# Attention and gated MLP on one core: the query projection by seven half-size products, with row blocks in two outer passes

## The chip, the cores and the metric

The kernel runs on one core of one Trainium2 chip. The metric is the device time of one execution in microseconds (us). Each kernel was run several times on the same chip beside the kernel before; "median" is the median of such runs. A ratio is the mean time of one kernel's fast runs over the mean of the other's fast runs of the same rounds, so it is not quite the ratio of the medians quoted. In the profile PE is the matmul engine (TensorE), PEld its weight loads, DVE is VectorE, ACT is ScalarE, POOL is GpSimd and SP is SyncE. "Clock" is the share of full speed that the PE's clock was granted.

## The reference

```python
xn = layernorm(x)                                  # x: (1, 2048, 640) bf16
q  = (xn @ wq)                                     # wq: (640, 32*192): 32 heads of 192
k, v = last 512 rows of the caches                 # 32 heads of 192
p  = softmax(q k^T / sqrt(192));  s = (p v) @ wo   # wo: (6144, 640)
g  = silu((sigmoid(xn @ w_gate) * (xn @ w_up)) @ w_down)   # 640 -> 1536 -> 640
return x + s * g
```

## The kernel before

First comes the gate network for all 2048 rows; its result goes to DRAM (`gB_d`). Then follow attention "runs". A run takes two blocks of 512 rows and one group of four heads. It has two halves: scores (with the query projection of the next run between the score tiles), then PV (with the output projection of the run before between the PV tiles). The head group is the outer loop and the row blocks are inside, so keys, values and weights of a group are loaded once.

Names that the profiles use: `ps_all` is PSUM, the eight banks in which PE's results build up; `hT_sb` is the hidden layer of the gate network; `gB_sb` is a row tile of gates on its way to DRAM and `gBa_sb` the same on its way back; `qp` is a product saved from PSUM; `k_sb` holds sorted keys and `kT` turned ones; `o_st` holds results of PV, which a DMA turns into `oT`; `o_sb` is a tile of output rows, ready for its store.

```python
def stage_q(n, u):                       # one tile of the projection: 20 matmuls = 10 pairs
    ...
    ps = bank2()
    for c in range(NCD):                 # 5 chunks of 128 of the 640 inputs
        for h in range(2):               # both halves of a chunk
            for b, r in enumerate((LO, HI)):      # upper and lower 64 rows of the array at once
                x = xnT if b == h else xnS        # xnS: the halves swapped
                nc.tensor.matmul(ps[:, b, :], lhsT=wq_t[g][r, 2*c+h, u::PC], rhs=x[s][r, c, :], ...)
    nc.vector.tensor_copy(qT_t[n][:, u, :, :], ps)
...
blocks = [(g, s) for g in range(NG) for s in range(NST)]
runs = [[n, n + 1] for n in range(0, last - 1, 2)] + [[last - 1], [last]]
...
def finish(ps, gB_sb, t, d0, d1):        # the last head group: gate, residual, store
    nc.vector.tensor_tensor(ps, ps, gB_sb[:, d], ALU.mult)
    nc.vector.tensor_tensor(o_sb[:, d], ps, acc[t][:, d], ALU.add)
    nc.sync.dma_start(of[t * P:(t + 1) * P, d], o_sb[:, d])
```

The softmax here doesn't subtract the row's maximum and nothing guards it: scores larger than these inputs give would overflow.

## Time and profile before

| | before |
|---|---|
| time, median | 929.75 us (929.44 to 930.16, 4 runs beside the changed kernel) |
| PE busy | 914.6 us, 99% of the span |
| DMA moved | 87.17 MB |
| one steady run (two halves) | 23.4 + 23.8 us |

These rows of the page cut the span into 40 slices. Each digit is the busy share of PE, the granted clock and the DMA share, in tenths.

```profile
PE   8999999999999999999999999999999999999997
PEclk9999999999999999999999999999999999999999
DMA  9534430144425342633454244434342434373655
```

PE has no hole between its ends and the clock stays at 0.9 or more. DMA is mostly near 40%. The list of PE's waits (waited for: us in total, times, longest) is correspondingly short; these are its two longest lines:

```profile
PE ps_all L413 <- DVE o_st L436: 1.4, 3, 0.9
PE ps_all L249 <- DVE warm L244: 1.3, 1, 1.3
```

### The profile page before, as it was taken

What the parts mean: (1) busy time and instruction counts of PE and PEld (TensorE: products, weight loads), DVE (VectorE), ACT (ScalarE), POOL (GpSimd) and SP (SyncE); (2) the same over time, 40 slices, a digit from 0 to 9 for tenths busy, and PEclk for the clock granted to TensorE, in tenths of its full rate; (3) what the DMA queues carried; (4) which work ended last, traced back from release to release, by engine and by line L of the source; (5) the groups of instructions that cost most, each with busy time, mean ns of one, the idle gap of its engine ahead of it and who ended that gap; (6) DMA issues with size and microseconds to landing.
All of it is one profiled execution on the core that took longest, in us unless ns stands there. A gap on an engine that the chain in (4) does not pass through costs nothing. (4 is left out here: it accounts for less than half of the span.)

```text
span 928.1 us, 18098 instructions
## 1 busy us (share of the span) xinstructions
PE 914.6 (99%) x7946; PEld 546.1 (59%) x8025; DVE 450.7 (49%) x639; ACT 302.1 (33%) x340; POOL 129.5 (14%) x170
## 2 busy tenths in 40 slices
PE   8999999999999999999999999999999999999997
PEld 5545445465756565656565656666665656566665
DVE  5443532443545454545454444444454545454477
ACT  4333322245141424242323333232323242424321
POOL 0021100010002000200020002000100010395800
PEclk9999999999999999999999999999999999999999
DMA  9534430144425342633454244434342434373655
GB/s 290 150 91 102 66 100 16 57 66 83 77 60 112 77 78 61 111 78 68 70 99 90 53 84 81 109 52 87 78 111 52 86 76 113 73 178 77 150 148 148
DMA packets 176960, 87.17 MB, mean 94 GB/s; under 512 B 152241, under 2 KB 171313, under 8 KB 176881
## 3 DMA queue, kind: packets, MB, share of 16 engines
q1 hardware_dynamic: 146864, 47.20, 26.3%
q0 software_dynamic: 6656, 22.81, 10.1%
q10 hardware_dynamic: 23360, 15.99, 6.2%
q8 instruction: 63, 1.03, 0.5%
q14 instruction: 17, 0.13, 0.0%
HBM read 44.70 MB, written 5.24 MB: 54 GB/s over the span
## 5 line engine op out<-in xcount | busy, mean ns | idle before, releaser
L417 ACT ACTIVATE E<-ps_all 128x1024 bf16<-128x1024 f32 x256 | 246.1, 1023 | 487.4 <-PE ps_all L413 372.1
L402 DVE CAST qT<-ps_all 128x1024 bf16<-128x1024 f32 x96 | 117.5, 1225 | 235.9 <-PE ps_all L397 233.4
L474 PE MATMUL ps_all<-wo_g,oT 128*128 128x128 bf16 (+2 forms) x1474 | 224.6, 296 | 3.3
L397 PE MATMUL ps_all<-xnT,wqp 64*128 64x512 bf16 x960 | 222.2, 376 | 0.3 <-DVE o_st L436 0.3
L397 PE MATMUL ps_all<-xnS,wqp 64*128 64x512 bf16 x960 | 221.4, 376 | 0.0
L429 PE MATMUL ps_all<-v_sb,E 128*128 128x193 bf16 x2048 | 190.3, 247 | 0.1
L413 PE MATMUL ps_all<-qT,kT 64*128 64x512 bf16 x1536 | 184.1, 376 | 1.4 <-DVE o_st L436 1.4
L429 PEld LDWEIGHTS <-E 128*128 128x128 bf16 x2048 | 168.5, 98 | 19.3 <-issue 7.2
L474 PEld LDWEIGHTS <-oT 128*128 128x128 bf16 x1536 | 121.5, 98 | 76.5
L397 PEld LDWEIGHTS <-wqp 64*128 64x128 bf16 x1920 | 100.4, 100 | 107.7 <-issue 0.8
L413 PEld LDWEIGHTS <-kT 64*128 64x128 bf16 x1536 | 74.7, 94 | 91.6 <-issue 6.4
L436 DVE TENSOR_TENSOR o_st<-ps_all,rden 128x768 bf16<-128x768 f32 x128 | 122.6, 958 | 8.3 <-DMA oT<-o_st 3.6
L507 DVE TENSOR_TENSOR acc<-ps_all,acc 128x640 f32<-128x640 f32 x96 | 79.2, 825 | 42.7 <-PE ps_all L474 42.7
L131 POOL COPY k_sb<-kn_sb 128x768 bf16<-128x768 bf16 x32 | 25.8, 831 | 273.5 <-DMA kT<-k_sb 225.9
L435 DVE RECIPROCAL rden<-ps_all 128x4 f32<-128x4 f32 x128 | 23.3, 182 | 81.2 <-PE ps_all L429 81.0
L326 DVE TENSOR_TENSOR hT_sb<-ps_all,sig_sb 128x512 bf16<-128x512 f32 x48 | 33.1, 692 | 51.0 <-PE ps_all L320 41.2
L152 POOL DMA_DIRECT2D wqp<-in_A_wq_dram x16 | 11.8, 741 | 319.4 <-PE ps_all L397 270.4
L320 PE MATMUL ps_all<-xnT,wu_sb 128*128 128x512 bf16 x220 | 55.6, 379 | 0.3
L320 PE MATMUL ps_all<-xnT,wg_sb 128*128 128x512 bf16 x220 | 55.5, 379 | 0.3
L340 PE MATMUL ps_all<-wd_sb,hT_sb 128*128 128x128 bf16 (+1 forms) x377 | 52.4, 298 | 0.4
L325 ACT ACTIVATE sig_sb<-ps_all 128x512 bf16<-128x512 f32 x48 | 28.5, 597 | 56.6 <-PE ps_all L320 56.2
L340 PEld LDWEIGHTS <-hT_sb 128*128 128x128 bf16 x384 | 29.7, 98 | 23.1
(49 smaller groups left out, 270.9 us busy)
## 6 DMA issues: line engine op xcount, KB each, us to landing
wqp<-in_A_wq_dram POOLq DMA_DIRECT2D x16, 480.0 KB, 6.4
wo_g<-in_A_wo_dram ACTq DMA_DIRECT2D x8, 960.0 KB, 5.9
kn_sb<-in_A_k_cache_dram POOLq DMA_DIRECT2D x32, 192.0 KB, 4.4
v_sb<-in_A_v_cache_dram ACTq DMA_DIRECT2D x28, 192.0 KB, 3.1
gB_d<-gB_sb POOLq DMA_DIRECT2D x16, 160.0 KB, 2.2
xnS<-xnT SPq DMA_DIRECT2D x8, 320.0 KB, 4.8
gBa_sb<-gB_d POOLq DMA_DIRECT2D x16, 160.0 KB, 2.8
xa_sb<-in_A_x_dram POOLq DMA_DIRECT2D x16, 160.0 KB, 3.1
```

Of the source, the lines that this page charges most:

```text
L320: nc.tensor.matmul(gu[:, i, :], lhsT=w[:, c, f * P:(f + 1) * P], rhs=xnT[s][:, c, :], start=(c == 0), stop=(c == NCD - 1),)
L325: nc.scalar.activation(sig_sb[:], gu[:, 0, :], AF.Sigmoid)
L326: nc.vector.tensor_tensor(hT_sb[:, f, :], gu[:, 1, :], sig_sb[:], ALU.mult)
L340: nc.tensor.matmul(oB_ps[:, d0:d0 + dsz], lhsT=hT_sb[:, f, q * P:(q + 1) * P], rhs=wd_sb[:, f, d0:d0 + dsz], start=(f == 0), stop=(f == NF ...
L397: nc.tensor.matmul(ps[:, b, :], lhsT=wq_t[g][r, 2 * c + h, u::PC], rhs=x[s][r, c, :], start=(c == 0 and h == 0), stop=(c == NCD - 1 and h ...
L402: nc.vector.tensor_copy(qT_t[n][:, u, :, :], ps)
L413: nc.tensor.matmul(ps[:, b, :], lhsT=kT[r, c * PC + j, :], rhs=qT[r, j, pp, :], start=(j == 0), stop=(j == PC - 1),)
L417: nc.scalar.activation(E_t[n, pp][:, c, :, :], ps, AF.Exp, scale=scale_qk)
L429: nc.tensor.matmul(o_ps[:, q // 2, q % 2, 0:DH + 1], lhsT=E[:, c, i, q * P:(q + 1) * P], rhs=vt[:, c, 0:DH + 1], start=(c == 0), stop=(c = ...
L436: nc.vector.tensor_tensor(o_st[:, :, i * DH:(i + 1) * DH].rearrange("p (b i) d -> p b i d", b=2), o_ps[:, :, :, 0:DH], rden[:].to_broadcas ...
L474: nc.tensor.matmul(oA[:, d0 - base:d0 - base + dsz], lhsT=oT_t[n, pp][:, q * PC + j, :], rhs=wo_t[g][:, cc, d0:d0 + dsz], start=(cc == 0), ...
L507: nc.vector.tensor_tensor(acc[t][:], oA[:, 0:D], acc[t][:], ALU.add)
```

## The change

The intent is to save matmuls. Take two row blocks, the two 64-row halves of each input chunk, and the two head pairs of a group. The projection is then a 2x2 by 2x2 block product, and Winograd's scheme does it with seven half-size products in place of eight, at the price of sums of rows (X) and of weights (T). The sums are kept in fp32r, with four bytes an element. The sums of rows have to stay in memory for a whole pass, so the row blocks become the outer loop: two passes of eight head groups.

```diff
+XA, XB, XC = (xnt_pool.tile([P, NCD, 512], FR, ...) for i in "ABC")        # sums of rows, fp32r
+TA, TB, TC = (wq_pool.tile([P, NCD, PC, P], FR, ...) for i in "ABC")       # sums of weights, fp32r
+    def sum_w(g, i, eng, eng2):            # per chunk group: GpSimd sums, one copy on ScalarE
+        tt(TB[:, cs], b(a,1,1), b(a,0,1), ALU.subtract)
+        tt(TA[:, cs], TB[:, cs], b(a,0,0), ALU.add)
+        tt(TC[:, cs], b(a,1,0), TA[:, cs], ALU.subtract)
+        tt(TA[HI, cs], b(HI,0,1), b(HI,0,0), ALU.subtract)
+        nc.scalar.activation(TB[HI, cs], b(HI,1,1), AF.Copy)        # or eng2.tensor_copy
...
-    stage_q: 6 tiles of 10 pairs per run, 6 casts of 128x1024
+    query_slots: 11 slots per run (ten of 5 pairs, one of 3), 12 copies and 11 adds of 128x512
+        s1: products with wb, X1 (bf16)      s2: TA, XA    s3: TB, XB    s4: TC, XC   (fp32r)
...
-blocks = [(g, s) for g in range(NG) for s in range(NST)]
+runs = [(pi, g) for pi in (1, 0) for g in range(NG)]
...
 in the gate network (stores unchanged on GpSimd), after the second row block:
+                for pp in range(G): load_kn((0, pp), pp); sort_k((0, pp)); turn_k((0, pp))
+                sum_w(0, 0, nc.gpsimd, nc.gpsimd); load_raw(0, 2, nc.gpsimd)
+                sum_w(0, 1, nc.gpsimd, nc.gpsimd); sum_w(0, 2, nc.gpsimd, nc.gpsimd)
...
 in every run, between scores and PV:
+            sum_w(g2, 0, nc.gpsimd, nc.scalar); load_raw(g2, 2, nc.scalar)
+            sum_w(g2, 1, nc.gpsimd, nc.scalar); sum_w(g2, 2, nc.gpsimd, nc.scalar)
...
+        if r > 0 and runs[r - 1][1] == NG - 1:
+            for j in range(4): load_gate(r - 1, j)        # nc.scalar, behind the copies above
```

## The prediction

> **What bounds the kernel now.** I read the page first: busy shares, then the costliest groups.
>
> ```profile
> span 928.1 us, 18098 instructions
> ...
> PE 914.6 (99%) x7946; PEld 546.1 (59%) x8025; DVE 450.7 (49%) x639; ACT 302.1 (33%) x340; POOL 129.5 (14%) x170
> ...
> L417 ACT ACTIVATE E<-ps_all 128x1024 bf16<-128x1024 f32 x256 | 246.1, 1023 | 487.4 <-PE ps_all L413 372.1
> L402 DVE CAST qT<-ps_all 128x1024 bf16<-128x1024 f32 x96 | 117.5, 1225 | 235.9 <-PE ps_all L397 233.4
> ...
> L397 PE MATMUL ps_all<-xnT,wqp 64*128 64x512 bf16 x960 | 222.2, 376 | 0.3 <-DVE o_st L436 0.3
> L397 PE MATMUL ps_all<-xnS,wqp 64*128 64x512 bf16 x960 | 221.4, 376 | 0.0
> ...
> L397 PEld LDWEIGHTS <-wqp 64*128 64x128 bf16 x1920 | 100.4, 100 | 107.7 <-issue 0.8
> ...
> L326 DVE TENSOR_TENSOR hT_sb<-ps_all,sig_sb 128x512 bf16<-128x512 f32 x48 | 33.1, 692 | 51.0 <-PE ps_all L320 41.2
> ```
>
> PE works all the time; every other engine mostly waits for it (the last column names PE). A shorter PE stream shortens the kernel only as long as PE keeps waiting for nobody. How long a projection matmul really takes is not the 376 ns of a row, since they overlap; the timeline of one tile of the projection (20 matmuls) shows the pitch:
>
> ```profile
> 404.74 0.59 PE L397 MATMUL ps_all<-xnS,wqp 64*128 64x512 bf16 x2
> 404.96 0.59 PE L397 MATMUL ps_all<-xnT,wqp 64*128 64x512 bf16 x2
> 405.18 0.59 PE L397 MATMUL ps_all<-xnS,wqp 64*128 64x512 bf16 x2
> ...
> 406.69 0.38 PE L397 MATMUL ps_all<-xnT,wqp 64*128 64x512 bf16 x1
> 406.90 1.46 PE L413 MATMUL ps_all<-qT,kT 64*128 64x512 bf16 x12
> 407.11 1.23 DVE L402 CAST qT<-ps_all 128x1024 bf16<-128x1024 f32 x1 [3.39 <-PE ps_all L397]
> ```
>
> From 404.74 to 406.90 ten pairs (upper and lower 64 rows at once) pass: 0.2155 us a pair. The scores that follow issue at once, and VectorE starts 0.21 us later. The windows of a steady run of two blocks show its two halves:
>
> ```profile
> 402.80:426.20 23.40, 23.40 (x217) 10.77 (x216) 8.06 (x7) 13.99 (x15) 1.60 (x2) 1.00 0.31 77
> 426.20:450.00 23.80, 23.59 (x222) 18.00 (x224) 15.01 (x24) 1.40 (x2) 0.00 (x0) 1.00 0.51 93
> ```
>
> Columns: stretch, length, busy PE, PEld, VectorE, ScalarE, GpSimd, clock, DMA. The first half is scores with projection (16 score tiles of 3 pairs, 6 projection tiles), the second is PV with the output projection. In both PE is full, at a clock of 1.00.
>
> **What the Trainium skill says.** "FP8 and Floating Point Precision", TensorE Precision Notes: reduced-precision fp32 is read as 4 bytes and truncated to FP22, while true fp32 takes 4 passes. I take fp32r to be one pass at bf16's pitch; the trace before holds no fp32r. "TensorE: Matmul & The Clock Gate", LDWEIGHTS and Weight-path perf modes: a load takes columns/1.2 GHz, which is 107 ns for 128, and the fast load isn't given to FP32. The bf16 loads agree with a faster one: in the PV half 16 of them go in 1.32 us, about 80 ns each. An fp32r pair needs two loads, estimated from that page at 213 ns, just under the 215.5 ns of its streams: hidden at best. The same page's specification table has ScalarE, VectorE and GpSimd as strict FIFO; the trace doesn't contradict it (ScalarE issues a load at 402.89 and only then starts the run's first exponential, at 403.70), though nothing there shows a blocked queue. "VectorE: DVE Perf Modes", Why PSUM operands drop a tier: fp32 from PSUM is 1x. The trace: 692 ns at 512 elements, 825 at 640.
>
> **The change, part by part.**
>
> Removed. Per run the projection had 6 tiles of 10 pairs, 60. Now there are eleven slots: ten of 5 pairs and a last one of 3 (its fifth chunk has no partner), 53. Over 16 runs 960 pairs become 848; 112 x 0.2155 = 24.1 us less. This is all there is to gain, 2.6%. Scores, PV, output projection and the gate network keep their matmuls.
>
> Added, evictions. 6 casts of 1225 ns become 12 copies and 11 adds of 128x512. At 692 ns that is 15.9 us instead of 7.4 per run, on an engine with 21.8 us in that half. It fits as a sum, but not as a chain. In Winograd's scheme a bank is saved and then accumulated further, so the next slot on the bank must wait. Head thirds 0 and 1 alternate on banks 4/6 and 5/7 and hide this; the last third has no partner. Independent VectorE ops follow at some 0.61 us (an estimate from 640-wide ones of 0.82 us that start 0.74 us apart), dependent ones 0.09 us after the end before; I allow 0.08 us back to PE. A score tile is 0.647 us. Then:
> - second product of the last third: 0.21+0.69+0.08 after the first, one score tile between: 0.34 us wait;
> - third product: two copies, 0.21+0.61+0.69+0.08=1.59, two score tiles (1.29) between: 0.30;
> - fourth: 0.98 against one score tile: 0.34;
> - first PV tile: its second bank waits for a copy and then an add (1.76) against a score tile and half a PV tile (1.31): 0.45.
> - Besides, scores now own banks 0-3 instead of a ring of eight, so the second score tile waits for the last output-projection tile's addition: 1.01 against 0.65: 0.36, in 13 runs.
> 15 x 1.43 + 13 x 0.36 = 26 us. This alone gives back the gain.
>
> Added, start. The first group's eleven slots have no scores between them. Before, the first cast could start only at 168.63, when the last gate store had landed, and PE had queued other banks; now the third slot needs that add. Walking the slots with 0.6 us ScalarE copies I get 18.5 us where there were 13.0: 7 us of waits on 11.4 of work. Then ScalarE's order in the second stage: before the first exponential stand a weight-sum copy, a load that waits for VectorE's four sums (about 4 us), a copy that waits for that load (3 us) and for four more sums (2.3 us), and a table load (1.28 us). The first exponential so comes about 15 us after the end of the prologue, while PE runs dry after two score tiles and one slot: 13.7 us.
>
> Added, beside other work. Weight sums on GpSimd: 12 per run, about 1.6 us for 768 elements (estimate from 1410 ns at 640), with the key sorting 18 us in a second half of 23.7 us: hidden, except in the first run, whose second half has no output projection (10.6 us): 2 us. K, V and wo are loaded twice and wq is loaded some 2.5 times as often: DMA was at 42% on average and goes to 60% or so: hidden. At the change of pass 4.6 MB of sums come back in one second half: 2 us. The x sums lie in the gate network's slack.
>
> Added, end. The last run has 16 score tiles and no projection beside them, before only 8: ScalarE's 0.93 us pitch against 0.65: 4.2 us.
>
> Sum: 929.6 - 24.1 + 26 + 7 + 13.7 + 2 + 2 + 4.2 = 960; I add 4 us for fp32r loads that show after a wait, since the load is then inside the instruction: **964 us**.
>
> **The rivals.**
> 1. *The saving arrives.* If the waits were half of mine and the queues ordered luckily: 929.6 - 24 + 20, about 925. For it: VectorE has 27% free in that half, and two thirds of the slots alternate banks. Against: the 0.98 us chain consists of measured durations. Faster than 911 needs waits under 6 us, which the prologue alone breaks.
> 2. *fp32r is slow.* 38 of 53 pairs per run are fp32r, 608 in all. If loads don't hide or the array takes two cycles a column, each pair costs up to 0.2155 us more: +131 us, about 1090. For it: no fast load for FP32, and 213 of 215.5 ns leaves no room. Against: one pass by the skill's page. Something between (pair of 0.25 us) gives +21, about 985.
> 3. *DMA or GpSimd becomes the bound*, the sums for the run after next not being ready when its second product starts: at 25 us instead of 18 per run about 1 us a run, 980.
>
> **Range and chances.** Bf16 pitch has about 0.65, then 945 to 975; a little slower 0.2, 975 to 1020; twice as slow 0.15. Faster by over 2% (under 911): 0.04. Within 2% (up to 948.2): 0.22, where my waits are half too large. Slower: 0.74. Range 938 to 1030.
>
> **What would show it.** Right: fp32r pairs at 0.216 us, PE busy falling by some 24 us, idle PE rising from 14 us to about 65, released by VectorE in front of the last third's products and the first PV tile; one hole of 10 us or more in the first run's scores with ScalarE waiting for a load; VectorE busy near 590 us (450.7 - 117.5 + 16 x 15.9). Wrong: a pair pitch over 0.23 us (rival 2), PE waiting for GpSimd in every run (rival 3), or VectorE waits under 0.5 us per run, when the time falls under 938.

## The result, and the profile after

The changed kernel takes 1073.58 us (1072.15 to 1075.64, 4 runs) against 929.75 us beside it: ratio 1.1548, 95% interval 1.1528 to 1.1568. It is 144 us slower. The direction was as predicted; the time lies outside the range of 938 to 1030.

The page of the changed kernel, its first lines and the same rows of slices:

```profile
span 1070.4 us, 18623 instructions
...
PE 944.3 (88%) x7706; PEld 607.7 (57%) x7785; DVE 597.6 (56%) x913; ACT 360.1 (34%) x401; POOL 520.8 (49%) x480
...
PE   9988929849799999999999992469999999999995
PEclk9999969869899999999999996679999999999998
...
DMA  8445650242839596696989583682959695984756
```

240 matmuls are gone, yet PE's busy time has risen, and its share fell from 99% to 88%. There are holes in slices 3 to 11 (the gate network and the first runs) and a large one in slices 25 to 27, where the second pass begins. In the slices of the large holes the granted clock is low too.

The list of PE's waits names who ended them, and the windows of one steady run show that the holes are not there (columns: stretch, length, busy PE, PEld, DVE, ACT, POOL, clock, DMA share, GB/s):

```profile
PE ps_all L612 <- DVE o_sb L622: 37.6, 3, 33.6
PE ps_all L555 <- ACT E L559: 19.2, 9, 13.6
PE ps_all L377 <- DVE gB_sb L409: 18.8, 1, 18.8
PE ps_all L555 <- DVE o_sb L622: 8.8, 1, 8.8
PE ps_all L401 <- DVE hT_sb L383: 5.7, 3, 2.5
```

```profile
568.70:592.60 23.90, 23.64 (x204) 14.12 (x202) 15.29 (x23) 14.98 (x15) 5.25 (x6) 1.00 1.05 197
592.60:616.50 23.90, 23.69 (x221) 18.01 (x224) 15.21 (x24) 3.25 (x4) 23.13 (x22) 1.00 0.61 122
```

A steady run takes 47.78 us against 47.23. So the change is nearly neutral there: of the 142 us between the two profiled spans only some 8 lie in eleven steady runs. I read the starts of the stages off PE's timeline in each trace and took differences (us):

| stretch | before | changed | difference | predicted |
|---|---|---|---|---|
| gate network, to the first projection matmul | 164.5 | 195.7 | +31.2 | 0 |
| first projection without scores | 13.0 | 22.9 | +9.9 | 5.5 to 7 |
| run 0 | 35.1 | 54.9 | +19.8 | about 16 |
| run 1 | 48.5 | 54.8 | +6.3 | as a steady run |
| PV of run 8 and scores of run 9 (change of pass) | 47.2 | 100.6 | +53.4 | as a steady run |
| last two runs to the end | 100.2 | 114.3 | +14.1 | 4.2 |
| the rest, eleven steady runs, with the reload of 4.6 MB (+1.5) | 519.6 | 527.2 | +7.6 | small |

**The change of pass.** ScalarE's timeline (start, length, instruction, idle before and what ended it) shows why the first output row of the first pass waited for its gate:

```profile
661.83 0.84 ACT L189 ACTIVATE TB<-raw 64x768 fp32r<-64x768 bf16 x1 [20.31 <-POOL TA L185]
...
671.16 0.84 ACT L189 ACTIVATE TB<-raw 64x768 fp32r<-64x768 bf16 x1 [8.48 <-POOL TA L185]
677.26 0.52 ACT L189 ACTIVATE TB<-raw 64x384 fp32r<-64x384 bf16 x1 [5.26 <-POOL TA L185]
677.32 9.03 ACTq L630 DMA_DIRECT2D gBa_sb<-gB_d  x7
```

The gate loads are issued at 677.3, directly after the third copy. Each copy had waited for a sum of GpSimd, which until 655.3 was preparing output rows. VectorE multiplied the first row by its gate at 679.66, after 36.5 us of idling, and PE, whose PSUM banks were full, went on at 681.48.

**The gate network.** GpSimd's timeline there, then PE's:

```profile
146.03 2.46 POOL L168 DMA_DIRECT2D raw<-in_A_wq_dram  x4
148.48 1.12 POOL L132 DMA_DIRECT2D kn_sb<-in_A_k_cache_dram  x2
149.59 1.08 POOL L411 DMA_DIRECT2D gB_d<-gB_sb  x2
```

```profile
158.86 2.29 PE L377 MATMUL ps_all<-x_odd,wg_sb 128*128 128x512 bf16 x5 [18.82 <-DVE gB_sb L409]
```

Two stores of gate rows were ready at 130.8 at the latest (VectorE's operation on the second began at 129.98 and took 0.82 us) but were issued only at 149.59, since they stood on GpSimd behind key sorting and weight sums. They landed at 158.0, and only then had the third row a free buffer (VectorE went on at 157.99, after 27.2 us). Nor does PE restart at full speed. The ten matmuls from 158.86 took until 163.08, 4.2 us; ten such just before the hole took 2.16 us.

PE also waited 7.8 us for `hT_sb`, all of it in the second row block. VectorE's multiplications stood there behind its first long sum of rows (GpSimd's sum, then VectorE's):

```profile
63.14 5.08 POOL L356 TENSOR_TENSOR XB<-x_even,x_odd 64x2560 fp32r<-64x2560 bf16 x1
63.27 7.64 DVE L359 TENSOR_TENSOR XB<-XA,xe_sw 64x2560 fp32r<-64x2560 f32 x1 [1.62 <-POOL XA L353]
```

VectorE's two other sums of this length took 2.8 us each. The first took 7.64 us, and it began just after GpSimd's second sum and ended 2.7 us after that sum. In the fourth row block it met only the last 0.8 us of GpSimd's and took 3.46 us. So VectorE seems to have stood still in it while GpSimd's sum ran; run 8 shows the same with shorter pieces.

### The profile page after: what moved, and what is told of

Its sections match the earlier page's. It is cut to its first block, busy times and chain, and to the rows that moved or that the text cites. A ratio compares the mean times of both kernels' runs of the same rounds, so it can differ in the third digit from the quotient of the medians.

```text
span 1070.4 us, 18623 instructions
## 1 busy us (share of the span) xinstructions
PE 944.3 (88%) x7706; PEld 607.7 (57%) x7785; DVE 597.6 (56%) x913; ACT 360.1 (34%) x401; POOL 520.8 (49%) x480
## 2 busy tenths in 40 slices
DMA packets 247797, 153.93 MB, mean 144 GB/s; under 512 B 196496, under 2 KB 236176, under 8 KB 246944
## 4 chain that ended last, share of the span: by engine, by line
PE 62%; POOL 14%; DMA 11%; DVE 6%; issue 6%; ACT 1%; SPq 0%; POOLq 0%; ACTq 0%; DVEq 0%
PE ps_all L469 18%; PE ps_all L612 13%; PE ps_all L555 12%; PE ps_all L569 11%; PE ps_all L377 4%; DMA gBa_sb<-gB_d 3%; PE ps_all L401 3%; DMA out_dram<-o_sb 2%; POOL TB L184 2%; DMA gB_d<-gB_sb 2%; POOL acc L604 2%; POOL TA L185 2%; POOL TA L187 2%; POOL TC L186 2%; POOL acc L605 1%
## 5 line engine op out<-in xcount | busy, mean ns | idle before, releaser
L612 PE MATMUL ps_all<-wo_g,oT 128*128 128x128 bf16 (+1 forms) x1380 | 214.9, 298 | 41.0 <-DVE o_sb L622 37.6
L555 PE MATMUL ps_all<-qT,kT 64*128 64x512 bf16 x1536 | 216.0, 385 | 33.6 <-ACT E L559 19.2
L184 POOL TENSOR_TENSOR TB<-raw 128x768 fp32r<-128x768 bf16 (+1 forms) x46 | 78.5, 1708 | 286.4 <-PE ps_all L469 282.6
L569 PEld LDWEIGHTS <-E 128*128 128x128 bf16 x2048 | 170.1, 98 | 22.5 <-issue 8.8
L488 DVE COPY qp<-ps_all 128x512 f32<-128x512 f32 x165 | 109.7, 688 | 88.0 <-PE ps_all L469 87.9
L501 DVE TENSOR_TENSOR qT<-ps_all,qp 128x512 bf16<-128x512 f32 x176 | 116.9, 688 | 57.4 <-PE ps_all L469 44.7
L469 PE MATMUL ps_all<-XA,TA 64*128 64x512 f32 x480 | 75.1, 436 | 6.5 <-DVE qT L501 4.2
L187 POOL TENSOR_TENSOR TA<-raw 64x768 fp32r<-64x768 bf16 (+1 forms) x46 | 78.8, 1713 | 3.6
L469 PE MATMUL ps_all<-XB,TB 64*128 64x512 f32 x480 | 79.0, 430 | 0.7 <-ACT qp L486 0.7
L186 POOL TENSOR_TENSOR TC<-raw,TA 128x768 fp32r<-128x768 bf16 (+1 forms) x46 | 70.3, 1528 | 3.6
L185 POOL TENSOR_TENSOR TA<-TB,raw 128x768 fp32r<-128x768 f32 (+1 forms) x46 | 69.4, 1510 | 3.6
L469 PE MATMUL ps_all<-X,wb 64*128 64x512 bf16 x480 | 63.6, 390 | 0.0
```

Of the source, the lines that this page charges most:

```text
L184: tt(TB[:, cs], b(a, 1, 1), b(a, 0, 1), ALU.subtract)
L185: tt(TA[:, cs], TB[:, cs], b(a, 0, 0), ALU.add)
L186: tt(TC[:, cs], b(a, 1, 0), TA[:, cs], ALU.subtract)
L187: tt(TA[HI, cs], b(HI, 0, 1), b(HI, 0, 0), ALU.subtract)
L469: nc.tensor.matmul(ps_all[:, b, :], lhsT=w(r, c), rhs=x[r, c, :], start=(first and k == 0), stop=(k == len(cs) - 1), skip_group_check=True,)
L488: nc.vector.tensor_copy(dst, part(b))
```

## The experiments

Fourteen runs of thirteen kernels gave results. All were correct. Times are medians in us; the kernel before took 929.84 to 930.10 beside them.

**1. Gate loads on SyncE.**

```diff
-        nc.scalar.dma_start(gates[t][:], gB_d[...])
+        nc.sync.dma_start(gates[t][:], gB_d[...])
```

> Edit: the loads of the saved gate rows (gB_d to gBa_sb) are issued by SyncE and no longer by ScalarE. Theory (in-order queues): in the changed kernel these loads are issued at 677.3 only because they stand on ScalarE behind three weight-sum copies that wait for GpSimd; the first output row of the first pass then waits 36.5 us for its gate and PE 33.6 us for VectorE. With the loads on SyncE that hole should fall to 0 to 12 us, the end should gain some us too, and the time should fall from 1073.6 to about 1040 (1030 to 1050). Rival (the 4.6 MB of sums that come back at the change of pass fill the DMA engines): the hole stays near 33 us and the time within 5 us of 1073.

Measured: 1069.01 (1058.84 to 1069.69). PE's long wait fell from 33.6 to 18.4 us, not below 12, in the profiled execution, which was the fastest (the other three took 1068.6 to 1069.7). The gain in time was only 5 us in the median, so my theory was half right. SyncE's own list of waits for that stretch shows what now stood in front of the gate loads:

```profile
SPq L147 <- POOL k_sb L140: 23.0, 1, 23.0
```

A transpose of keys stood on SyncE ahead of them and waited 23.0 us for keys that GpSimd sorted only after it had prepared the output rows (at 654.6). It was issued at 656.25, and the first gate loads at 658.88. One queue had hidden another.

**2. All gate stores on ScalarE.**

```diff
-                nc.gpsimd.dma_start(gB_d[...], gB_sb[:])
+                nc.scalar.dma_start(gB_d[...], gB_sb[:])
```

> Edit: the stores of the gate rows (gB_sb to gB_d) are issued by ScalarE and no longer by GpSimd. Theory (in-order queues): the gate network ends 31 us later in the changed kernel because the stores of its third and fourth row block stand on GpSimd behind key sorting and weight sums; the buffer gB_sb comes free late, VectorE waits 27 us for it and PE 18.8 us for VectorE, and some 2 us are lost to a lowered clock after it. With the stores on ScalarE the network should end near 171 to 176 us in place of 195.7 (the waits of the second row block, about 8 us, stay) and the time should be 1048 to 1055. Rival (the slowness in that stage comes from VectorE's and GpSimd's x sums or from DMA traffic as such): the end of the network moves by less than 8 us.

Measured: 1076.26, no gain. The 18.8 us wait was gone, but PE now waited 7.0 us for a gate weight at the start and 8.4 and 6.5 us for transposed rows. GpSimd's timeline tells why:

```profile
1.46 3.16 POOL L155 DMA_DIRECT2D v_sb<-in_A_v_cache_dram  x4 [0.16 <-issue]
```

In the changed kernel this load of values was issued at 51.80, behind the fourth gate store. The stores had been holding the attention's loads back. Without them the loads start at 1.5 us, before most of the gate network's own weights.

**3. Only the late gate stores on ScalarE.**

```diff
-                nc.gpsimd.dma_start(gB_d[...], gB_sb[:])
+                (nc.gpsimd if s < 2 else nc.scalar).dma_start(gB_d[...], gB_sb[:])
```

> Edit: the stores of the gate rows of the third and fourth row block are issued by ScalarE; those of the first two stay on GpSimd, where they hold back the loads of keys, values and weights that stand behind them. (With all of them on ScalarE the earlier run showed these loads already at 1.5 us, in front of the gate network's own weights, and new PE waits of 7.0 and 8.4 us for DMAs.) Theory (order on GpSimd's queue, both ways): the 18.8 us wait of PE for gB_sb goes and no wait at the start comes; the last matmul before the projection falls from 195.7 to about 172 to 178 and the time to 1049 to 1057. Rival (stage limited by DMA traffic of the saved sums and key loads): it moves by less than 8 us, with PE waiting for DMAs instead.

Measured: 1054.61, 19 us faster. The gate network ended at 180.0 in place of 195.7, and the first projection took 18.2 in place of 22.9 us, since its second add no longer waited for the last gate store. The end of the network is 2 us later than I expected: 11.0 us of waits for VectorE's `hT_sb` remain, where VectorE does the long sums of rows or waits for GpSimd's.

**4. ScalarE free ahead of the first run's scores.**

```diff
-    for i in range(3):
-        sum_w(1, i, nc.gpsimd if i == 1 else nc.vector, nc.scalar)
-        if i == 0: load_raw(1, 2, nc.scalar)
...
+    sum_w(1, 0, nc.vector, nc.vector)
+    load_raw(1, 2, nc.sync)
+    sum_w(1, 1, nc.gpsimd, nc.gpsimd)
+    # sum_w(1, 2, nc.vector, nc.vector) after the third score tile of run 0
```

> Edit: in front of the first run's scores ScalarE no longer makes copies for the second head group's weight sums nor issues their third load (copies go to VectorE or GpSimd, the load to SyncE); the third sum is emitted after three score tiles. Theory (in-order queue of ScalarE): the 13.6 us in which PE waits for the first exponential fall to under 4 us and the time falls by 7 to 12 us, to about 1064 (some of it comes back because VectorE has more to do there). Rival (the hole comes from the missing queries, that is from VectorE's chain or fp32r products, not from ScalarE's order): the hole stays over 10 us, the time within 3 us of 1073.6.

Measured: 1063.78 (1062.53 to 1068.64), 9.8 us faster. PE's longest wait for an exponential fell from 13.6 to 3.2 us, and the first half of run 0 from 41.4 to 35.0. ScalarE's order was the cause of the hole; part of it came back as a wait of 4.4 us for VectorE, which had been given the copies, and whose second sum now stood among the scores.

**5. Projection slots spread unevenly.**

```diff
-            if done < len(q_list) and (k + 1) * (len(q_list) + 1) >= (done + 1) * len(s_list):
+            if done < len(q_list) and k in (1, 2, 3, 4, 5, 6, 7, 8, 10, 12, 13):
```

> Edit: only the places of the eleven projection slots among the sixteen score tiles change: the first eight directly one after the other, two score tiles ahead of the last third's second product and of its fourth. Theory (VectorE chains of the last third set the waits): the waits there, about 0.7 us per run in the changed kernel, mostly go, and with 15 runs the time falls by 6 to 12 us, to about 1064. Rival (the steady state is lost to fp32r pairs that are slower than bf16 pairs, 0.233 against 0.216 us, and the waits hide under them): the time stays within 4 us of 1073.6, and the pairs keep 0.233 us.

Measured: 1064.98 (1059.12 to 1068.12), 8.6 us faster. A steady run went from 47.78 to 47.25 us. So part of its time was VectorE's chain in the last third. PE's timeline of this run also shows the rival's term side by side, since score tiles (12 matmuls, partly split over two lines) and slots alternate without waits:

```profile
518.34 0.83 PE L555 MATMUL ps_all<-qT,kT 64*128 64x512 bf16 x6
518.98 1.26 PE L469 MATMUL ps_all<-X,wb 64*128 64x512 bf16 x10
520.06 0.83 PE L555 MATMUL ps_all<-qT,kT 64*128 64x512 bf16 x6
520.52 1.53 PE L469 MATMUL ps_all<-XA,TA 64*128 64x512 f32 x10
521.88 0.84 PE L555 MATMUL ps_all<-qT,kT 64*128 64x512 bf16 x6
```

A score tile with a bf16 slot takes 520.06 - 518.34 = 1.72 us, with an fp32r slot 521.88 - 520.06 = 1.82 us. Five fp32r pairs thus cost 0.10 us more: with 0.647 us for the score tile, 0.235 us a pair against 0.2155. Taken from the single starts in this trace, pairs within an fp32r slot follow one another by 0.233 us in the median, and by 0.216 within a bf16 slot.

**6. Preparation and gate loads moved.** The first two loads of the preparation stand before the weight sums, the others and the gate loads on SyncE.

```diff
+        if early: prep_load(r - 1, 0); prep_load(r - 1, 1)      # GpSimd, before sort_k and sum_w
...
+        if early:                                               # at the end of the run
+            for j in range(2 * TQ):
+                prep_sums(r - 1, j)                             # GpSimd
+                if j + 2 < 2 * TQ: prep_load(r - 1, j + 2, nc.sync)
+            for j in range(4): load_gate(r, j)                  # nc.sync
```

> Edit: for the change of pass, the first two loads for the preparation of the output rows stand on GpSimd before the weight sums, the other six on SyncE, and the gate loads on SyncE after them. (With the gate loads alone on SyncE the earlier run still had an 18.4 us wait: their buffers were held by this preparation on GpSimd, which ended at 654.6.) Theory (GpSimd's queue: 1.1 us of issue per row and 7.4 us of wait for the first load make the preparation 15 us longer than its sums): the preparation ends near 640, the wait falls under 5 us, run 8's second half from 66.8 to about 40 us (the waits for the stores of output rows stay), the time to 1035 to 1050. Rival (DMA engines full at that place): the wait stays over 15 us.

Measured: 1050.31, 23 us faster, at the edge of what was expected. The edit also took the gate loads out from behind the key transpose, which run 1 shows as their last wait; the note above blames the buffers instead. The preparation ended at 645.9 (expected 640), PE's first wait there was 0.7 us, and the PV half of run 8 fell from 66.8 to 46.7 us (expected 40). The next half stayed at 32.7 us, now with a wait of 13.7 us for `o_st`.

**7. Sums in bf16.** Less exact on purpose; the result still passed as correct.

```diff
-FR = mybir.dt.float32r
+FR = mybir.dt.bfloat16          # and the DRAM copies of the row sums in bf16
```

> Edit: all sums in bf16 in place of fp32r, in their DRAM copies too; the result may be less exact, that is on purpose. Theory (an fp32r slot of five pairs costs 0.1 us more than a bf16 one, 7.6 such slots a run): a score tile with a slot falls from 1.82 to 1.72 us in every slot, the first half of a steady run from 23.87 to 23.1 to 23.5 (part is taken by VectorE chains), and with quicker x sums in the gate network and half the reload the time falls by 10 to 25 us, to about 1055. The large holes stay. Rival 2 of the prediction (fp32r pairs at twice the time): the time falls by over 100 us.

Measured: 1044.35, 29 us faster, a little more than I had allowed. A steady run takes 22.85 + 23.95 = 46.80 us, 0.98 less than with fp32r. The gate network shortened by 11 us: PE's waits for `hT_sb` fell from 7.8 to 3.3 us and that for `gB_sb` from 18.8 to 14.4. The large holes stayed (66.4 us for the PV half of run 8). The groups of the projection's line show what differs on PE in the steady run (ns min/median/max, then first and last start in us, forms). With fp32r, in the changed kernel:

```profile
L469 PEld LDWEIGHTS ps_all<-XA,TA x480: 182/185/334, 197.7 to 974.4; 64*128 64x128 f32 x160
L469 PE MATMUL ps_all<-XA,TA x480: 383/393/985, 197.7 to 974.6; 64*128 64x512 f32 x160
```

With bf16, in this run:

```profile
L469 PEld LDWEIGHTS <-TA x480: 92/94/148, 186.7 to 946.4; 64*128 64x128 bf16 x160
L469 PE MATMUL ps_all<-XA,TA x480: 372/376/631, 186.9 to 946.6; 64*128 64x512 bf16 x160
```

The weight load doubles from 94 to 185 ns. Over fifteen projections the 0.98 us make 15 us. It is not the 131 us of rival 2: 38 pairs at double pitch would add 8.2 us to the first half of every run.

**8. Together:** runs 3, 4, 5 and 6, and VectorE's three long sums of rows cut into fifteen pieces.

> Edit: late gate stores on ScalarE, the preparation and gate loads as in the run before, ScalarE free in front of the first run's scores, slots spread unevenly, and VectorE's three long x sums cut into fifteen pieces. Theory (losses are separate in time, so gains add): 1073.6 - 22 (gate stores) - 30 (gates) - 9 (first run) - 8 (spread) - 7 (x sums) = about 998, 985 to 1010. The steady runs stay at 47.25 us, so that nothing is left of the 24 us that were to be saved. Rival (the holes are symptoms of one shared limit, GpSimd or DMA, and move on when one is closed): above 1020.

Measured: 1023.23 where I expected 998. The rival, that the holes move on, was right for one of them; and cutting the sums of rows, from which I expected 7 us, gave nothing. The gate network ended at 181.7 (180.0 in run 3). The first of the fifteen pieces took 5.5 us in both row blocks and ended 0.6 us after GpSimd's sum beside it; the others took 0.7 us each. The PV half of run 8 fell from 66.8 to 41.1 us, but the half after it rose from 33.9 to 41.0. SyncE's queue in that stretch:

```profile
646.99 10.23 SPq L589 DMA_TRANSPOSE oT<-o_st  x1
657.31 1.52 SPq L633 DMA_DIRECT2D out_dram<-o_sb  x2
658.94 8.65 SPq L589 DMA_TRANSPOSE oT<-o_st  x1
669.43 0.34 SPq L633 DMA_DIRECT2D out_dram<-o_sb  x1
```

Output rows stand behind transposes whose issue alone takes 10.2 and 8.7 us (2.9 and 1.7 us for the two before); during these two the DMA share is 1.07 and 1.15. Output rows have two buffers. VectorE waited 30.6 us in five waits for them, and PE for VectorE.

**9. Output stores on ScalarE**, with that run's copies and its third weight load on GpSimd, so that the loads of the next values come after the stores.

```diff
-        nc.sync.dma_start(of[...], o_sb[:, d])
+        eng.dma_start(of[...], o_sb[:, d])          # nc.scalar in the first pass
-            sum_w(g2, 0, nc.gpsimd, nc.scalar)
+            sum_w(g2, 0, nc.gpsimd, cp)             # cp = nc.gpsimd in the run after the pass
```

> Edit: the combined kernel, with the stores of the first pass's output rows issued by ScalarE in place of SyncE (where they stood behind oT transposes that took 10.2 and 8.7 us to issue), and in that run the copies of the weight sums and the third weight load on GpSimd so that ScalarE waits for no one; the loads of the next values then come after the stores. Theory (what is left of the change of pass is a queue behind full DMA engines: run 8's two halves took 41.0 and 41.0 us against 23.8 and 23.4): run 8's second half and run 9's first half fall together from 82 to 50 to 60 us and the time from 1023 to about 1000. Rival (the DMA engines are full there whatever the order, shares of 0.92 to 1.10): the two together stay above 72 us and the time above 1013.

Measured: 997.07. The two halves together fell from 82.1 to 59.3 us. The bytes are the same (153.93 MB in both); the issuing order decided, not the amount to move, although the DMA share was above 1 in places. The edit moved three things at once (stores, copies, a weight load); what each is worth wasn't measured.

**10. The order of the loops alone.** The kernel before with two passes and head groups inside; eight products, no sums.

```diff
-    blocks = [(g, s) for g in range(NG) for s in range(NST)]
+    blocks = [(g, 2 * p + i) for p in range(2) for g in range(NG) for i in range(2)]
+    # wq of the group after next, K and V of the next group loaded in every run
```

> Edit: the kernel before with only the order of its blocks changed to two outer passes with head groups inside, as in the changed kernel, each group's keys, values and weights loaded once per pass; eight products in bf16, no sums of rows or weights. Theory (most of the loss comes from the sums: their place in the queues of GpSimd, ScalarE and VectorE, not from the order of the loops): steady runs stay at 23.4 and 23.8 us, the change of pass costs under 15 us, and the time is 932 to 950. Rival (the order of the loops with its doubled loads and its output rows in the middle is what costs): over 970, with a hole of over 25 us at the change of pass.

Measured: 1111.30, slower even than the changed kernel, with PE waiting about 8 us in every run for `o_st`. This looked like the rival, but the trace showed a fault of my own: both key transposes stood on SyncE ahead of the PV transposes, and the second waited for keys loaded only there.

> Edit: the earlier run with the order of the loops alone lost 8 us in every run by a fault of mine, not by the order: both key transposes stood on SyncE in front of the transposes of the PV results, and the second waited for keys that were loaded only there. Now the keys of a run are loaded one run ahead and the second transpose stands in the middle of PV, as in the changed kernel. Theory (the sums and their place in the queues cost most of the loss): steady runs at 23.4 and 23.8 us, the change of pass under 15 us longer, time 932 to 955. Rival (the order of the loops with its doubled loads costs by itself): over 970, with waits in every run or over 25 us at the change of pass.

Measured: 977.10, 134 us less, only by loading keys earlier and moving the transpose. It was still above my 955: about 2 us of waiting for the exponentials in most runs. ScalarE's load of output weights, which must wait for PE, stood in front of four value loads, and these (3.8 us of issue) in front of the first exponential.

```diff
+        for hp in hps: load_v(hp, nc.scalar)
         if r > 0 and blocks[runs[r - 1][0]][0] != g: load_wo(g)
-        for hp in hps: load_v(hp, nc.scalar)
```

> Edit: as the last run with the order of the loops alone, but ScalarE issues the loads of values before the load of the output weights, as in the changed kernel. In the last run the output-weight load waited for PE and held the four value loads back; their issue took 3.8 us in front of the first exponential, and PE waited 2 us in most runs for it. Theory (that wait is again my order on ScalarE's queue, not the loops): with it gone the steady runs are at 23.4 and 23.8 us in most runs, the time 940 to 955 from 977, so that the loop order itself costs 10 to 25 us of the 144. Rival (the doubled loads by themselves hold the exponentials back): the waits stay, the time over 965.

Measured: 945.72 (944.48 to 945.87), ratio 1.0164, interval 1.0147 to 1.0181. Steady runs are back at 23.4 + 23.8 us. What remains is mainly two waits:

```profile
PE ps_all L402 <- DMA wqp<-in_A_wq_dram: 5.7, 2, 3.9
PE ps_all L479 <- DVE o_sb L489: 4.7, 1, 4.7
```

The loop order, with its doubled loads, thus needs to cost no more than 16 us of the 144 (1.6% above the kernel before, which is clear of the noise).

**11. Run 9 in bf16**, with six buffers for saved products and for output rows, and the sums of rows one stage later.

> Edit: the kernel with the output stores on ScalarE, with all sums in bf16, six buffers in place of four for saved products and six in place of two for output rows, x sums one stage later. Theory (bf16 pairs at 0.216 us, waits hidden by the spread): a steady run's halves at 22.3 to 22.7 and 23.8 us against 23.4 and 23.8 before, so that the saving shows there at last, about 1 us a run or 13 us in all; the time about 975 (960 to 990), still above the kernel before since the start, the first runs and the end keep some 50 us of waits. Rival (DVE chains, not fp32r, hold the first half): it stays at 22.8 or more.

Measured: 966.12, 966.47 and 972.92 us in three executions (the next note says 966 to 970); the fourth, the one profiled, took 3494.94 us with PE busy for 3442. Its trace shows PE alone slow, in every stage: matmuls of 512 columns in the gate network start 0.84 us apart, against 0.216 in the later profile, while VectorE's busy time is the same (590.7 against 589.7 us). I don't know why and leave it out. Once more for a profile:

> The same kernel as the combined one in bf16; its profile fell into one execution of 3495 us while three others took 966 to 970. This run is for a profile in the fast state only: time 966 to 971; a steady run's halves at 22.3 to 22.7 and 23.8 us if fp32r's slower pairs were what hid the saving, 22.8 or more for the first half if the waits for VectorE's copies and sums hold it (rival).

Measured: 968.17. Steady runs take 22.56 + 23.81 = 46.37 us, 0.86 less than in the kernel before. Here the saving shows at last. The rival (VectorE's chains hold the first half at 22.8) is out for this arrangement, though some waiting must remain: without any, 112 pairs less over sixteen projections would give 1.5 us. No version came below the kernel before. In this one run 0 and the first projection are 18 us above it, the change of pass 14.5 (61.7 against 47.2), the last two runs 12.4 (112.6 against 100.2) and the gate network and run 1 together 2.9, against 9.3 us gained in the eleven steady runs.

## Why the prediction was right or wrong

**Right: what is saved and what eats it.** Seven products save about 1.5 us per run and waits give most of it back. In the steady run the net was +0.55 us. The spread of slots (run 5) took 0.53 us off it, so VectorE's chain was there. With bf16 (run 7) the saving of 1.51 became 0.43, so about 1.1 us of waits remain per run, where the prediction's chain summed to 1.43 + 0.36. That term was too large by some 0.7 us a run. With the spread, more buffers and bf16 (run 11) 0.65 us remain; I haven't traced them.

**Right: the hole in the first run.** Predicted 13.7 us, measured 13.6, before the exponentials. Run 4 confirmed ScalarE's order as the cause. That the number agrees so well is luck: VectorE's first four sums took 7.5 us and not 4, the load 4.4 and not 3, the wait for the next sums 1.2 and not 2.3, and PE, at a low clock, ran dry later. The sentence was the only place where the prediction walked a queue instruction by instruction.

**Undersized: fp32r.** "I add 4 us for fp32r loads that show after a wait" was the term; the runs show 0.98 us per run, some 15 us. My estimate of two loads in 213 ns, one after the other, was wrong in both parts: one load takes 185 ns, and the two of a pair run side by side. In the trace of run 5 they start 10 to 21 ns apart, as the prediction's own line could have told me for bf16 (1920 loads of 100 ns in 100.4 us of busy time). So a pair grew by 0.0175 us only, to 0.233; whether the load or the stream sets that pitch no run here shows. 38 such pairs are 0.67 us of the 0.98. The 0.3 us left, 4.7 us in fifteen runs, may be the loads after waits that the term meant (an estimate from these numbers); what it left out was the pitch. By its own sign (over 0.23 us a pair) rival 2 was met in kind but not in size.

**Wrong: "The x sums lie in the gate network's slack."** They don't. VectorE does its part in three pieces of 2.8 to 7.6 us, and PE waited 7.8 us in the second row block for tiles that VectorE had not multiplied. Cutting them up did not suffice in run 8: VectorE waited for GpSimd's first sum (5.9 us in both row blocks together) and then stayed in its own first piece, 5.5 us each time, while GpSimd's second sum ran. No run was made for this stall alone. The quicker bf16 sums, placed later, brought the end of the network to 166.6 us in run 11.

**Wrong: "At the change of pass 4.6 MB of sums come back in one second half: 2 us."** The size was right, 1.5 us in run 6. But the change of pass has a second place, the first pass's output rows in run 8, and that cost 53.4 us. The prediction had no term for it.

**Wrong: the gate stores.** The prediction counted GpSimd's weight sums where they meet attention, not where they stand in front of stores of the gate network. So the buffers of the stores came free late: VectorE waited 27.2 us for one, and PE 18.8 us for VectorE. With the sums of rows this came to +31.2 us, of which run 3 took back 15.7.

**The end.** Predicted 4.2, measured 14.1. The scores of the last run took 15.44 us against 10.4 at full pitch (16 tiles of 0.647), which is the predicted mechanism at about 5 us. A 3.7 us wait for `o_st` and a later last store (8.5 us after PE's last matmul against 5.0) come on top; the remaining 2 us I have not traced.

**The failed step, in one sentence:** the prediction treated each addition as time on an engine, "hidden" when the engine had room, and asked for its place in the queue only in the first run. Of the 110 us by which 964 was too low, the change of pass makes some 53 and the gate network 31; both terms were 0 or 2. VectorE's share was right: it was expected near 590 us and came to 597.6. GpSimd's was not: 12 sums and the key sorting take 22.5 us a run, not 18, and issuing its loads another 4.7, so that it is busy for 23.13 of 23.90 us in the second half. At 49% of the whole span it still delayed everything that stood behind its sums. Moving issues and a few copies to other places and queues, with the sums of rows cut in pieces, took the kernel from 1073.6 to 997.1 us (run 9); the arithmetic and the fp32r sums stayed.

**Rival 3, partly right.** "DMA at 60% or so: hidden" holds in the steady run, although its first half reaches a share of 1.05. On the whole the queues took 67% (43% before): `wq` is loaded about five times as often, by the pages' lists of loads, and not 2.5 times. At the change of pass some issues became slow, up to 10.23 us for a transpose. There a new order helped with the same bytes, so DMA was not the bound; how much the traffic added to the late transfers no run separates. PE did not wait for GpSimd in every run, the sign of this rival. Rival 1's sum, too, was loose: half of the prediction's waits (59 us with the 4 us for loads) gives about 935 and not 925, unless one counts on luck.

**PE's busy time** was expected to fall by 24 us and rose by 30; its idle time was expected near 65 us and came to 126. Busy time is not a count of work. With bf16 it was 922.0 us (run 7), and with most holes closed as well 915.2 (run 11): in the traces fp32r matmuls (393 against 376 ns) and matmuls after a hole at a low clock (4.2 against 2.16 us for ten) are longer. That run 11 still doesn't show the 24 us I haven't traced.

**What stays open:** the one 3495 us execution, VectorE's stall beside GpSimd's sums, the rest of the end, and whether an arrangement exists that beats the kernel before. The best steady run gains 0.86 us, which would be 13 us if all fifteen runs did. The loop order alone cost about 16.

## What to carry to other kernels

Before adding work to an engine that has room, list what stands behind it in the same queue, above all stores, loads and copies, and ask what each of them holds up; 49% busy is no protection, least of all when the engine is nearly full in the half where others wait for it. A transfer that waits in a queue also holds back the transfers behind it, sometimes to good effect, so check what starts earlier when it is moved. A saving of 2.6% on the bounding engine leaves no room for such mistakes: price the pipeline's ends and changes first, since the steady state was the only place where the prediction's sums came close.

## What the Trainium skill lacked or had wrong

- "TensorE: Matmul & The Clock Gate", LDWEIGHTS: columns/1.2 GHz, 107 ns for 128 columns, is not what fp32r takes. It was 185 ns, against 94 to 100 ns for bf16. That no fast load is given to FP32 agrees. I found fp32r's pitch on no page: 0.233 us for a pair against 0.216 in bf16. (The precision notes cited in the prediction give four passes for true fp32; that fp32r takes one was my reading of them, and this pitch fits it.)
- "DMA: Bandwidth & Descriptors", Anatomy of one DMA: it says that a semaphore wait happens on the issuing sequencer before dispatch. The runs agree (in run 1 SyncE stood 23.0 us at a transpose that waited for GpSimd's keys, with the gate loads behind it), and I should have used it. What it lacks is that issuing can itself become slow: in run 8 one transpose took 1.73 us to issue and the next of the same size 10.23, while the DMA share was 1.07, and it held the stores behind it. Its section Issuing engines are not separate DMA queues says that issuing from several engines only saves issue time, which is usually small. In that stretch it wasn't small, and in a queue with waits more than issue time is at stake: the same bytes, with the stores on another queue and some copies moved too, took the change of pass from 82.1 to 59.3 us.
- "GPSIMD Engine Reference", Elementwise: it has a two-input operation on fp32 at about half VectorE's speed. I found no figure for bf16 inputs with fp32r output: 5.1 us for 2560 elements on GpSimd (2.0 us for 768 in the weight sums), and 2.8 us for 2560 on VectorE with one bf16 input, when GpSimd did not run a sum beside it.
